# Same operations and fetches in another order on all engines

## The chip, the cores and the metric

One core of a Trainium2 chip runs the kernel. The time is what the device takes for one execution, in microseconds, as the median of several. All five engines work beside each other, each through its own queue in its own order, and wait for each other by semaphores: TensorE (PE in the profile; PEld is its loading of weights), VectorE (DVE), ScalarE (ACT), GpSimd (POOL) and SyncE (SP), which here only issues loads and stores.

## The reference

Two stages, all in float32. First an attention over a sliding window with a bias that falls with distance, for 8 batches, 8 heads, 576 positions and 64 columns a head; then, on its result with the heads side by side (512 columns), a mixture of 4 experts of which each position uses 2. Each expert is itself a causal attention of 64 columns.

```python
scores = scale * np.matmul(q, k.transpose(0, 1, 3, 2))
mask = (rel >= 0) & (rel < 128)
scores = np.where(mask, scores + bias[None], -1000000000.0)
attn = softmax(scores);  x = attn @ v            # then heads side by side: B, 576, 512
logits = x @ w_gate;     topk = the 2 largest of 4;  w = softmax over these 2
for e in range(4):
    q, k, v = x @ wq[e], x @ wk[e], x @ wv[e]
    ye = softmax(causal(scale * q @ k.T)) @ v @ wo[e]
    out += (w of e where e is in topk, else 0) * ye
```

## The kernel before

The attention goes by groups: a group g is a pair of heads of one batch, so there are 32, four to a batch; positions are cut into four tiles of 128 and a tail of 64. For a group PE forms scores (tiles `s`), DVE lays the window together (`copy_predicated`), adds the bias and finds the maximum in one custom operation (`p<-s,tbt`), ACT takes the exponential and its sum, DVE sums and inverts (`tensor_reduce`, `reciprocal` into `r`), POOL or ACT scales `p`, PE transposes it (`t`), DVE or ACT copies it to `pa` (one copy is multiplied by a mask, `pa<-t,tmt`), PE multiplies by the values (`x`), and the result is stored as a rounded part and the rest (`xh`: a copy, then a difference). Groups 0 to 3 at the start are handled in two halves, A (tiles `sA`, `pA`, `tA`, `paA`, `xA`) and B with the tail C (`sB`, `sC`, ...).

The experts' part works on a batch of four groups: projections to q and k (`qk`, stored to `QSm` and `KHm`, again as a part and a rest), to v and the gate (`v`, `lg`), scores (`ms`, tail `msl`), softmax (`mp`), transposes (`mt` to `mpt`), values (`ma` to `AHm` and `ALm`; the tail `mal` to `AHTm` and `ALTm`), and the output projection (`o` to `ot`), which is stored. The weights of all projections are split as well: `WH` is the rounded copy of the staged `wst`, `WL` the difference, by `wprep` (line 1006).

Heads are 64 wide, so many matmuls use only half of the array's columns (the values, `x` and `ma`, two at a time on the two column halves) or half of its rows (scores of the first groups). A change between such a tiling and the full array is a change of array tiling.

The program is first recorded, not issued: `_Rec` (line 188) stands in for the engines, and every call of line 201 on is put into a list. Where two engines could do an operation, `nc.any` (line 195) records both alternatives: copies from PSUM to SBUF (`evac`, line 218: ACT or DVE), rounding and scaling (`rnd`, `scl`, lines 222 and 227: POOL or ACT), differences (`ssub`, line 236: DVE or POOL). `plan` (line 158) then turns the list into the real order. It unpacks the constant `ORDER` (line 39), which holds one entry for every instruction of the whole kernel: twice the number of the operation plus 0 or 1 for the alternative, or a negative number for a fill, a matmul on a zero tile whose result nobody reads (`warm`, line 411). Two matmuls on the two halves of the array make one entry (`_pairs`, line 145). The last lines issue what comes out:

```python
    seq_ = plan(nc.ops, nc.alt) if K["mode"] else nc.ops
    for e, m, a, k in seq_:
        getattr(getattr(tc.nc, e), m)(*a, **k)
```

That is why every row of the profile names line 1276, and why rows are told apart by the tiles they write and read. The order of one engine is the order of its entries; only semaphores tie the engines to each other. Tiles come from pools with a fixed number of buffers, so an entry that writes a buffer waits for the last reader of what was in it.

Loads go mostly through SP: the e tiles (q and k of groups 0 to 7), `vt` (values), `wst` (weights), `mtt` (a mask), from group 8 on `r` and `tl`, and the stores of `ot`. POOL's queue fetches `h` and the copy of `wo`.

Of the kernel before, what the change touches and what calls it, by code (L numbers as in the profile page):

```python
# [19 lines left out]
B, H, S, D = 8, 8, 576, 64  # L20
DM = H * D
E = 4
P = 128
NP_ = H // 2
# [14 lines left out]
    "c-pmjeOzl-m3GcKD<8LTO>Ck`P1>ZAX{bblB^_uJC#gvVZ_<J#l_<Fb78G7V!G@N!V1q&nQ>b7;!9s-!N=BH0npm(w!2yMzprFKp1_gx*dg%)m"  # L39
    "6f8K*-us*cTHAU5dIRJn=j_k5o@cFRZBhYJfxI+%BBLfRU9U{-D9~hgSSoxXLrUQ!Skel0;-o^IxvRChN*ox<mvwDOZM7SD`ibbq%MYuUSF5H!"  # L40
    "{_5h^rRy}sj|<9tryu!~$(FP~`{AF=I_p4}r_$tYRg1sNd$i7CYUp1pfpBT<je^R>hSIM*XmCHoBd>S0zUy&MdO^T&dlK(U@X1e0bk!ZEt5=dd"
    "6(7It_V2X+W#i7~)cnFdcdh38PZrfy7+Q)F!IM|&^M37mIFjvvzu{W7#PPSs(lYDp-PN_m_r9&U>++@D@YEk4aQyDYik-~i&W6U8bTicKxA~M0"
# [1321 lines left out]
```

## Time and profile before

| | us |
|---|---|
| runs | 545.03, 545.17, 545.23 |
| median | 545.17 |
| the profiled execution, its own time | 545.23 |
| its span on the core | 543.5 |
| busy: PE, DVE, ACT, POOL | 532.0, 451.4, 424.7, 348.8 |
| granted clock of PE over the span | 1.00 |

Busy time is a sum over an engine's instructions; that of PE is modelled, as matmuls are pipelined, and bars of DVE overlap the next one by some 0.08 us. A row of the timeline gives the start, the time, the engine, the line, the operation, what it writes and reads with its shapes, how many in succession were put together, and in brackets the idle time of the engine ahead of it with the engine and tile that ended it.

### The profile page before, as it was taken

The page shows a single profiled execution, that of the slowest core. Times are in us where ns is not written, and L with a number is a line of the kernel's source. Part 1 is how long each engine was busy: PE and PEld are TensorE (multiplying, and loading weights), DVE is VectorE, ACT ScalarE, POOL GpSimd, SP SyncE. Part 2 cuts the span into 40 slices and gives each one's busy share as a digit, 9 for nine tenths or more (in the row PEclk, how much of TensorE's full clock was granted, in tenths as well). Part 3 has the DMA queues.
Part 4 walks back from the last instruction along what each step waited for, and adds up shares of the span by engine and source line. Part 5 has one row for each costly group of instructions (what it writes and reads, how often), then busy time and mean ns, then how long its engine had stood idle before and what let it go on. Part 6 is the DMA issues. An engine that isn't in the chain of part 4 may idle for free.

```text
span 543.5 us, 13708 instructions
## 1 busy us (share of the span) xinstructions
PE 532.0 (98%) x4353; PEld 453.9 (84%) x4353; DVE 451.4 (83%) x1945; ACT 424.7 (78%) x1477; POOL 348.8 (64%) x591
## 2 busy tenths in 40 slices
PE   6899999999999999999999999999999999999997
PEld 4688877897898878899788987889789898898875
DVE  4899898989887888898988888878998889866852
ACT  4877888978988888976979769867798977665782
POOL 2644577788766766576596687865669666632640
PEclk9999999999999999999999999999999999999999
DMA  7963424354533547416436354435445240200013
GB/s 201 252 189 109 155 74 145 132 163 160 200 128 98 175 143 239 157 59 199 141 123 201 119 202 149 148 107 175 162 156 169 81 161 24 76 21 2 19 60 98
DMA packets 30376, 72.99 MB, mean 134 GB/s; under 512 B 3168, under 2 KB 11360, under 8 KB 30304
## 3 DMA queue, kind: packets, MB, share of 16 engines
q1 hardware_dynamic: 22752, 42.69, 25.1%
q0 software_dynamic: 6672, 28.84, 16.2%
q8 instruction: 35, 0.57, 0.4%
q10 hardware_dynamic: 880, 0.59, 0.4%
q14 instruction: 37, 0.30, 0.2%
HBM read 62.67 MB, written 9.44 MB: 133 GB/s over the span
## 4 chain that ended last, share of the span: by engine, by line
PE 92%; DVE 3%; DMA 3%; issue 1%; SPq 0%; ACTq 0%; ACT 0%; DVEq 0%
PE qk L1276 19%; PE s L1276 11%; PE v L1276 10%; PE o L1276 9%; PE x L1276 8%; PE ms L1276 7%; PE mt L1276 7%; PE ma L1276 7%; PE t L1276 5%; PE msl L1276 2%; PE mal L1276 2%; PE xt L1276 1%; DMA e<-in_rd 1%; PE mtl L1276 1%; DVE pa L1276 1%; DMA tbt<-in_tb 1%
## 5 line engine op out<-in xcount | busy, mean ns | idle before, releaser
L1276 POOL TENSOR_TENSOR h<-r,h 64x512 fp32r<-64x512 f32 x96 | 122.9, 1282 | 16.7 <-DMA r<-in_rd 9.9
L1276 PE MATMUL qk<-xh,WH 128*128 128x288 f32 (+2 forms) x512 | 123.0, 312 | 0.4 <-DVE ot L1276 0.3
L1276 ACT ACTIVATE p<-p,nm 128x128 f32<-128x128 f32 x252 | 99.3, 396 | 14.4 <-DVE nm L1276 12.8
L1276 PEld LDWEIGHTS qk<-xh,WH 128*128 128x128 f32 x512 | 85.0, 189 | 5.2 <-issue 1.6
L1276 POOL TENSOR_SCALAR mp<-mp,mr,w 128x512 f32<-128x512 f32 (+3 forms) x128 | 76.1, 604 | 16.9 <-DVE mr L1276 9.8
L1276 ACT ACTIVATE mp<-mp,mnm 128x256 f32<-128x256 f32 (+3 forms) x128 | 71.1, 557 | 13.5 <-DVE mnm L1276 12.9
L1276 PE MATMUL qk<-xh,WL 128*128 128x288 f32 (+2 forms) x256 | 76.8, 307 | 0.0
L1276 PE MATMUL s<-h 128*128 128x256 f32 x336 | 72.8, 299 | 0.0
L1276 POOL TENSOR_SCALAR p<-p,r 128x128 f32<-128x128 f32 x131 | 47.4, 368 | 36.6 <-DVE r L1276 13.2
L1276 PE MATMUL ms<-KHm,QSm 128*128 128x256 f32 (+2 forms) x224 | 69.0, 359 | 0.1
L1276 DVE TENSOR_TENSOR pa<-t,tmt 128x512 f32<-128x512 f32 (+2 forms) x84 | 64.3, 773 | 5.6 <-PE t L1276 3.7
L1276 PE MATMUL v<-WH,xh 128*128 128x260 f32 x288 | 65.2, 294 | 0.0
L1276 ACT COPY mpt<-mt 128x384 f32<-128x384 f32 (+1 forms) x84 | 44.1, 534 | 26.6 <-PE mt L1276 25.1
L1276 PE MATMUL mt<-idt,mp 128*128 128x128 f32 x320 | 60.9, 273 | 0.0
L1276 DVE CUSTOM_DVE_ANT_0 mp<-ms,mtt 128x256 f32<-128x256 f32 (+2 forms) x96 | 52.4, 552 | 8.1 <-PE ms L1276 7.5
L1276 PEld LDWEIGHTS s<-h 128*128 128x128 f32 x336 | 53.3, 189 | 3.7 <-PE ma L1276 0.4
L1276 DVE CUSTOM_DVE_ANT_0 p<-s,tbt 128x128 f32<-128x128 f32 x204 | 53.2, 284 | 1.9 <-issue 0.2
L1276 PE MATMUL x<-pa,vt 128*64 128x256 f32 x448 | 51.6, 359 | 0.1
L1276 DVE COPY_PREDICATED s<-mkt,s 128x256 f32<-128x256 int32 (+2 forms) x140 | 45.0, 330 | 6.3 <-PE s L1276 4.4
L1276 PE MATMUL t<-idt,p 128*128 128x128 f32 x252 | 49.7, 273 | 0.1
L1276 PEld LDWEIGHTS v<-WH,xh 128*128 128x128 f32 x288 | 48.2, 189 | 1.9 <-issue 1.3
L1276 ACT ACTIVATE p<-p,r 128x128 f32<-128x128 f32 x121 | 45.4, 396 | 5.0 <-DVE r L1276 3.7
(180 smaller groups left out, 1381.4 us busy)
## 6 DMA issues: line engine op xcount, KB each, us to landing
h<-in_hd POOLq DMA_DIRECT2D x24, 1152.0 KB, 5.8
r<-in_rd SPq DMA_DIRECT2D x24, 576.0 KB, 4.2
vt<-in_vd SPq DMA_DIRECT2D x28, 320.0 KB, 3.8
out<-ot SPq DMA_DIRECT2D x31, 256.0 KB, 3.3
e<-in_hd SPq DMA_DIRECT2D x18, 128.0 KB, 4.4
wst<-in_wall SPq DMA_DIRECT2D x4, 386.0 KB, 5.1
tl<-in_hd SPq DMA_DIRECT2D x24, 64.0 KB, 3.4
out<-ot SPq DMA_DIRECT2D x8, 128.0 KB, 2.4
```

The source lines that it names most:

```text
L1276: getattr(getattr(tc.nc, e), m)(*a, **k)
```

## The change

Only the constant `ORDER` is replaced, a packed text of 99 lines; all code and all operations stay.

```diff
@@ -36,105 +36,105 @@
 ORDER = (
-    "c-pmjeOzl-m3GcKD<8LTO>Ck`P1>ZAX{bblB^_uJC#gvVZ_<J#l_<Fb78G7V!G@N!V1q&nQ>b7;!9s-!N=BH0npm(w!2yMzprFKp1_gx*dg%)m"
...
-    "#iJI*A^6Q46+4lp-s(RMZ*2U({RiTI>2t0n{=dKe2iG*+_5"
+    "c-pmjeOzm2mG1sn`8Z89X-RJwK}k*8#6nG4Vu=lH(uOgdk~V2!3<?!&Q0PE~7TTmG7A#ayuwWAlE%AT@Eli;UmP|oGgMxxWg%K(!+=2rNQ>dVD"
...
+    "b0|A&(9>s+MC;~g!#`^2%hoxo&S?6a<F0O~(*KYDAwivQLA|e6&l7^7|C<i}|EJgg1ypak>H"
 )
```

Unpacked, the list has 6483 entries instead of 6482. The one more is a fill (14 instead of 13; the fills stand among the first 55 matmuls in both). 384 operations take their other alternative: POOL to ACT 123, ACT to POOL 117, ACT to DVE 74, DVE to ACT 62, POOL to DVE 5, DVE to POOL 3. An entry stands at another place of its engine's list for 2877 of 3192 entries of PE, 1470 of DVE, 977 of ACT, 563 of POOL and 94 of SP. On PE the column-tiled runs move as wholes and in parts, mostly by about a microsecond of PE's own work, at most by 18 us later or 8 earlier.

At the start the two lists look like this on DVE (operation, tile written, tiles read; the numbers are places in the engine's list, counted from 0):

```text
place  before                                after
28     minimum pA2 <- sA2                    copy paA <- tA0
29     minimum pA2 <- sA3                    split paA <- tA0,tmt
37     split paA <- tA1,tmt                  copy paA <- tA1
40     tensor_reduce r3 <- sm                tensor_reduce r3 <- sm
41     copy xh1 <- xA1                       reciprocal r3
42     copy WH <- wst0                       difference WL <- wst0,WH
43     difference WL <- wst2,WH              copy WH <- wst3
44     reciprocal r3                         difference WL <- wst1,WH
45     difference xh1 <- xA1,xh1             copy WH <- wst1
50     copy_predicated sB0_1                 difference xh1 <- xA1,xh1
56     difference xh2 <- xA2                 copy_predicated sB0_1
```

ACT gives the copies to paA of tA0, tA1 and tA3 to DVE, and three of its scalings to POOL; three copies to WH come to it from POOL. Its exponentials of one group stand closer together. On PE the transposes of tA3 come ahead of the first sC instead of behind the values xA2. On SP the first 19 loads are the same; then come, before, vt0, vt1, four e2, vt2, vt3, e4, e6, vt4 and so on with mtt at place 43, wst4 at 44 and tl8 at 46; after, tl8, vt0, vt1, e2, mtt, three e2, vt2, wst4 (place 28), vt3, e4, e6, e6, vt4. On POOL's queue the load of h for group 8 comes ahead of that of wo. In the last microseconds the cast of AHTm for the last tail is put on ACT, behind a copy to ot.

## Rows read from the trace of the kernel before

**Rows 1.** The page: busy time of PE with its share of the span and its instructions, and the chain that ended last, by engine.

```profile
PE 532.0 (98%) x4353; PEld 453.9 (84%) x4353; DVE 451.4 (83%) x1945; ACT 424.7 (78%) x1477; POOL 348.8 (64%) x591
PE 92%; DVE 3%; DMA 3%; issue 1%; SPq 0%; ACTq 0%; ACT 0%; DVEq 0%
```

**Rows 2.** Busy time by stretches. Columns: the stretch, its length, busy time and instructions of PE, PEld, DVE, ACT and POOL, the granted clock of PE, the busy share of the DMA engines, and GB/s.

```profile
6.20:20.00 13.80, 11.30 (x65) 8.55 (x66) 10.37 (x62) 10.31 (x44) 7.67 (x18) 1.00 0.95 268
20.00:37.00 17.00, 17.00 (x151) 13.18 (x150) 15.86 (x73) 13.60 (x55) 10.70 (x20) 1.00 0.68 183
37.00:60.00 23.00, 23.00 (x207) 19.12 (x206) 20.92 (x100) 17.86 (x74) 7.13 (x16) 1.00 0.51 153
60.00:84.30 24.30, 23.85 (x194) 18.98 (x193) 22.79 (x104) 19.66 (x75) 18.62 (x37) 1.00 0.33 107
...
100.00:540.00 440.00, 439.28 (x3627) 379.88 (x3623) 367.31 (x1551) 348.30 (x1181) 290.79 (x476) 1.00 0.39 127
```

**Rows 3.** The chain of waits, 83 to 86 us: start, us, what.

```profile
84.08 0.09 DVE ws L1276
...
84.23 0.70 PE ms L1276 x2
```

**Rows 4.** Timeline of PE, 74.4 to 78 us.

```profile
74.97 1.77 PE L1276 MATMUL x<-pa,vt 128*64 128x256 f32 x16
76.67 0.38 PE L1276 MATMUL ms<-KHm,QSm 128*128 128x256 f32 x1
76.98 0.45 PE L1276 MATMUL xt<-pa,vt 128*64 128x64 f32 x8
```

**Rows 5.** Groups of instructions of DVE with shapes kept apart: busy time, mean ns of one, idle time before them.

```profile
L1276 DVE COPY pa<-t 128x256 f32<-128x256 f32 x9 | 3.7, 414 | 0.0
...
L1276 DVE TENSOR_TENSOR WL<-wst,WH 128x256 fp32r<-128x256 f32 x2 | 0.8, 414 | 0.0
```

**Rows 6.** Timeline of DVE, 8 to 20 us: the reductions that wait.

```profile
10.79 0.16 DVE L1276 TENSOR_REDUCE r<-sm 128x4 f32<-128x8 f32 x1 [0.91 <-ACT pA L1276]
...
16.09 0.16 DVE L1276 TENSOR_REDUCE r<-sm 128x4 f32<-128x8 f32 x1 [0.68 <-ACT pA L1276]
...
18.79 0.16 DVE L1276 TENSOR_REDUCE r<-sm 128x4 f32<-128x8 f32 x1 [1.08 <-ACT pA L1276]
```

**Rows 7.** Timeline of ACT, 8.5 to 21 us: two exponentials.

```profile
10.28 0.38 ACT L1276 ACTIVATE pA<-pA,nmA 128x128 f32<-128x128 f32 x1
...
18.25 0.41 ACT L1276 ACTIVATE pA<-pA,nmA 128x128 f32<-128x128 f32 x1
```

**Rows 8.** The chain of waits from 0 to 40 us (first row) and the timeline from 19.6 to 23.5 us (the others).

```profile
12.35 7.33 DMA e<-in_rd
...
19.82 0.56 PE L1276 MATMUL sC<-e 128*128 128x192 f32 x2 [0.69 <-DMA e<-in_rd]
...
21.96 0.76 DVE L1276 COPY_PREDICATED sB<-mkt,sB 128x256 f32<-128x256 int32 x2 [0.50 <-PE sB L1276]
...
22.62 0.66 PE L1276 MATMUL tA<-idt,pA 128*128 128x128 f32 x4
```

**Rows 9.** Timeline of DVE, 49 to 67 us: waits for PE, and one for ACT.

```profile
49.13 0.43 DVE L1276 COPY_PREDICATED s<-mkt,s 128x256 f32<-128x256 int32 x1 [0.21 <-PE s L1276]
...
56.90 0.49 DVE L1276 COPY_PREDICATED s<-mkt,s 128x128 f32<-128x128 int32 x2 [0.22 <-PE s L1276]
...
59.90 0.76 DVE L1276 COPY_PREDICATED s<-mkt,s 128x256 f32<-128x256 int32 x2 [0.41 <-PE s L1276]
...
62.97 0.16 DVE L1276 COPY lg<-v 128x4 f32<-128x4 f32 x1 [0.78 <-ACT v L1276]
...
65.69 0.29 DVE L1276 COPY_PREDICATED s<-mkt,s 128x128 f32<-128x128 int32 x1 [0.29 <-PE s L1276]
...
66.70 0.29 DVE L1276 CUSTOM_DVE_ANT_0 p<-s,tbt 128x128 f32<-128x128 f32 x1 [0.25 <-PE t L1276]
```

**Rows 10.** Issues on SP's queue, 18 to 32 us, the sB matmuls of group 2 on PE, and from the page the median time from issue to landing of such a load (last column).

```profile
18.03 0.60 SPq L1276 DMA_DIRECT2D e<-in_rd  x1
19.70 0.60 SPq L1276 DMA_DIRECT2D e<-in_hd  x1
...
31.28 0.33 SPq L1276 DMA_DIRECT2D vt<-in_vd  x1
...
27.14 1.13 PE L1276 MATMUL sB<-e 64*128 64x256 f32 x8
...
e<-in_hd SPq DMA_DIRECT2D x18, 128.0 KB, 4.4
```

**Rows 11.** Timeline of all engines, 536.5 to 543.6 us.

```profile
536.99 0.22 DVE L1276 CAST AHTm<-mal 128x64 fp32r<-128x64 f32 x1 [2.61 <-PE mal L1276]
...
537.54 0.37 ACT L1276 COPY ot<-o 128x256 f32<-128x256 f32 x1 [0.59 <-PE o L1276]
...
538.06 0.29 PE L1276 MATMUL o<-WOH,AHTm 128*128 128x256 f32 x1
```

**Rows 12.** Timelines of POOL, 15 to 18.5 us (first two rows), and of DVE (the last).

```profile
15.49 0.77 POOL L1276 TENSOR_SCALAR WH<-wst 128x256 fp32r<-128x256 f32 x2 [0.56 <-DMA wst<-in_wall]
...
16.97 1.00 POOL L1276 TENSOR_SCALAR WH<-wst 128x260 fp32r<-128x260 f32 x2
...
17.29 0.41 DVE L1276 TENSOR_TENSOR WL<-wst,WH 128x256 fp32r<-128x256 f32 x1
```

More of the change, by code (lines that the diff above doesn't have):

```diff
@@ new lines @@
+    "1qJ24@4I(6oYVPZ?jJY5kmT(B?)PJ@=UMAn>lgqGKwc`h*r;-+Bq@S<sv47RL0?tY9!^eWWvO|ptdKpVO{oZV+lJ)cBK`DSRzvQ<^jdf9dg0n&"
+    "$7GTJy-(N1R>qy&`fx#w20kV*rWJqu$v}Y-D)j>{*(a!{vwbp;KkH`?=X~hF!omq#o31xUntZaWdXA!Ac;e{>*IU1Qi2Bg+rv!4r#rv(F%#PGb"
+    "uX)@KpSWYt|5zf0Ua#s6-dpaS&1@`cPQ2~!O$N}n78&P%`{J$NFG^B+gYD{2V^grQ8cu(3dn5eupAGlDnU$VkcT{9v|6H?5@~)sJWQeO-Gqi-v"
+    ")`sQ}KQrSIl>w}JmP|go^=mK2l<4<9@J5p%$v@xxz$de{`Op+hZ7;G`Wj=6QUGtA_2%5G2m_Xk_0~E^q<5MZ?YjxEFH6hJZ&00$8dORymNd?f3"
+    "?Euszy3z{);+5!1PFeAQ<&o@*^s8-q6;FIxp^4Gxt8=b>xr(h9N&Agebs9rr&q!Kof4HGquRmxC0+baS68&Dt&IDEJWK+Jm?6G^r*~x(pxbV*G"
@@ new lines @@
+    "a6;#r`qr1r)4%XhNYdVN8z^L|I8eo%9BLA*k`oE6&rI%Yss@Lr5;{SfG&TZ|Y}(0inKw=0*rC0Dd}S%&`a2d!4Y$6&wLWm|Z4PsbqY)s+)LQD>"
+    "eDPw(@m^E)64WG*LQSH<mJX2NLhnqe1HSXBGb=Dt6Yo%Fo2~BnSRI;ua>i4nH#)@$b*cqt_5Rc;0?-pruWsZOz~V}RX8#Dx@yf)Kj|r8o%G>X-"
+    "DW*%S*W$MOQZL*H;cwoOyPTjAS-oj7D*&>zIhZcB!nC5a8a&eJjS=W-hu7bLPzz*c2U|inzF?C=Ot>&PsiHsp?VrN_ku1<7Q?yJhLH|HoQbPb-"
+    "r_j)7U4>U)Z0g?GoO|pyp<`-$Z})(O;m)3+(Y6qbXdMZ^__X)BdqmpIdb2&Rpi40*Z4F3zx(_UJkjP<LGpE+|TH@<+x8s)^lk0P`q1-pKo7SF>"
+    "Z5(mcsZGA}&7H2iaJjGCa&qT~`viB}gHQh8jk~6mJNva;dgErLuVH^;Xeax^%@M8Dd?fRX&K9Tktr|}DYZqOR9PDb>)MREuXJ=3WDb3!UWU+py"
@@ new lines @@
+    "VXhBudj#x;TBYpzkEO*m8~l5ou5g2|f85hkYfAM@heuM55|^cs33skUerTFN{xqy1|93CgOM}qcB@Kj^*JcM4^4TKj?kkur>r<P>^1--{8*etq"
+    "a<x!Vd}7;KU0L5+&aQ`J>b>9lo6&g#tq`+*GC7kFkFK3&C1^5DD)`Lj)H(zRb*jYr-8TzMY%Oa&F|pl!`#0RA*2xsCxXqGQEN&@07%?VVWo?EA"
+    "Q{<_;Hih>dYz<B+cjZl*gbY_nVIxdin@x)=@Vj>b%186#lG?>d`4;KVzgvFN7F&P#EF*3@)Fn3Ol!?F<nc6a2or>gX>$c}KtK65l0=BiD={Z}4"
+    "@IHxL0Y-b+Gi40)fAM+{4HP#IA@kY$MsnTbePUbp9{le=NGz4QRyZC`hhs-L<HO%C^7Oc4(@(nljw#5v^;r<vT$$M-DXWZ!Q>(eXWLmb?q$z{s"
+    "{A`5Ryn>vW<ucDV|Ef27jH+@UNIkh)Yu5NwAnPf?L{so*pY|bS{Op~kYOl20mkw&5b78lOE!ZnN4VJ;~!Q_nghhG9X1+TxXT)YbQTK{6HF%Uvi"
@@ new lines @@
+    "w>K*gBia)tAfjABbWz4n4l9<EO<>Ogun&b{aA#p8tkg(Mb3<Y2{N~=&>0mHk+7D|}Z2%LI)<9{!uTres%G)Z|R8GBj;bgGLl2+GPToz|9%24Y("
+    "pSnB#XKzG`9{tbeVsm`+$c3MmRul#|+d2R`d&B*%jQWm|vC4nFIoVtNm9M7T-u{ho$g{nNtU&b+By5TyPIVZNj3u0`9wwGFEsA5}5hi2`mw(bS"
+    "yE0c=QCcytNO|Nx=ONeK+~7=?2G^mnZm=;U>qn1|&c~1T4~LWqYIi|S?r&-Jn7s@If`kf~KKj<n%CM!h!WyHs23jp?W;U&N1DW+3cV$^*MwQd("
+    "4t9L%zKNgwGgKO-sVQD5BKq`4?oX-KXH;+6?I<`ydHvqD)D)WSf$cr;u4yNVZuwgCL>A1Oon>*>wL;<dOk2yZerKhj$1ILlrVW4elW1J==n;xn"
+    "$5dUTO#`dUr#0R&=i~pDQc+p4djens!?wlZZC$p=4q!b#dB!MO-s&CLjEz}7ST6gIUj?pxC-bAX&r%DA)~$7m2H-@z9WymPH5+d~JQ>;h@Vn`@"
@@ new lines @@
+    "4o}ZVo^>khF3HIet$ndQ^|;{Doqhf8)<F9YE|g^b?O972o8<0Wjx}31=V5f{B(b6{9eJxMXcs$!?Iqx}F7EVB#Ku%nl?sUQD>qCCBXKH#bekb@"
+    "+hPEnyAd{@f9j^UJoR3Qh$^n!DX!crMd7v~@9SR#3!A={paE9Ai84&GLz`ekkv%6rx#$=7)xzA-?i{G5lIJz`f=lKhfN)LdcdKu-0JwA2Q_$H1"
+    "@U`bpI|{z@s;9`Ei@3msPH${|G--S)(eT)-;3*nXnUW1jCRRKJiH3SavCJ&UF@y@cl9HOrHCfH>B+&TEQD|V*{(;`X?hXIo@av!LhVMQg?vj-S"
+    "T62nL%6*l=xX@t=n0z~4zeilw;IHvHMXk;W*QDPxyPz1KiHUWmfn@gpAPsEt?!IXh_2(cNZ4>tTc3=6S8Z-%T+~AjkOrcQ1sc{Ziom`SAUQ9HU"
+    "JN|OV)Z|$A()>W@BhM#5u&FsRY!GkX_j?yBotqxF!{$!TGe4^_7Ua3E|I(17%q@4=+gWjB!lmr%+;%Fna<xgBJ@<SGoG9;0`k=k5XV78pbd=VG"
@@ new lines @@
+    "J9-WqC6&6x6)ja&3%A_Xn-+>w#UZ8`r@EU}Co!>bDn3!`jth#1?T(Bbk@O&<2Wk2*sxMZQHrDiISZCr-w|@DAPODr)%(Y8`(xLUBC1^jCDLX95"
+    "4aT7_JRdYBw&cQde+8T0?(tcuWM_7xZE&Ty%r@R!B8fk}`?E2+CHv$|=XdUPX4!xLy0x#{a^3IJi**G}!Gw@)=GWgZF3^jUitDqL4b7G`eOK9b"
+    "tv9r~Av-d`u-6Z%`_DXe(BPWL?wr~`8uz)jCsu9ZLDPh-$Xx|XO=VgB28&8rK3v<Y)NJm^5$+C8?te)~nTJO6SN_irM{KEw@qx61WTQ^O&Mcza"
+    "p0&^3E|NA$(%`dqD#5Y>{o8x`HJwr+)+SBQN#v1<*#((m(iuO$6q$%SumU@wqvl1Tt)v)GCXVds)BIk46;yi*OMH;!oX$13nR8Dvm$df^w%n1R"
+    "?K6LddSvXP-dF^UmHYnWSu3A$=H!c{Gn*<fCn-SPJv?ZySgNm?g#*yGA`t-QreMsamnK2puvd^ONz1ONvO54_rlNc{Js~q&3nxj7^);<0lA0a1"
@@ new lines @@
+    "CHzmH44Zoj2MzThc<LP#6!mF)01eFueupP^S7CvD*r2u!H(S_Vqdq?grXRZ}v4EYs_YZpG`j%vIi|FCQB@N8O4X=SRFi<I*v%u*@BsHb35d~Sb"
+    "E&z%l)2=u>b88)3a*^~ee??iKZncCJcaN6^bjR$(zg_Hr@!3|GZOA|MHO?;Nm73POBqay&dFdDLkJT!wG;>|;<zAl;pi)tS>{Ta?i7oei;0qZ$"
+    "OXa?8#mayEAx=F}-4YM2NK_??M@A~t;Z}Ek4vJ8=^kWL0<=5}P@*2uB(}(+sTOy<VrrVBKyTUZbMzS*}D7L+49Cq}E%^j!eZ!baX$mnSxrY}(B"
+    "sh^yijufYEX%^+*x~|(Q%PjI}YQOz2?%Z+z=dZCtWFp&Bv|%3avj2_23D+@_e^dm{R-{jxN+GpjXw;Q4G*C)a91aaT>@ffL-x%AfV`7bZ({`Us"
+    "AyJrCWJi&eE$AJ9<@att@yAt{x)Bh!b+~gu7MbYK&e<AcO6x~VKGBR*otin(I$Ni;R=B?RgK*u1^%M?4l0FWh?Sm6}IR)m$ShKTv`pfrQeDJrg"
@@ new lines @@
+    "($8$}RLb&q65~y>`d*jl$M?o1H?K9^{G6v}T;=GrrN@*=tw#;bt7-BQW&R47t)2cPz3dZDn=AS|yS!tFExGRe2i{K7PUPmL2bw1e<}+9^Ol5!d"
+    "y{gXUWssQvaC<`5TwHmdOe94a@dMY{9qLuf29ki11KX1iOM=d!z9q0qVl5`iAo7c6E!EMdUyg-8|FP!~>5h@H{n1O;+77zQhDJ@@eYxrxu%zuC"
+    "%rC9V6l=?RV}{DWipw7P6557$!Ch55Xk3~Hzc-_``)Hloa%Q*=Cp;sXIF(u#bL9N@mtp<iFXe>?^1}Vlgrc{n@nr4ByGvm8;-6sqzPq}56`?>A"
+    "G&el_kaH?#7$8A2c$x*;(%44m7uCY9ZEVD7$Q-bmpL}w&W5n+bHZ;38vYnIG%6A^3_Qe_m<o2%RH6+=O6HLxv6N06I<fWO#MDhO7GD=hBsZK+#"
+    "TeYCp+4_$F#l?)Gtw5`2IBO`;0L!U$joQkuJh?MI)!qe<J=vnusjK!*TU-t#bllo9@qU`+`VUzLU^j29XnwG9@?fxWd}?}bIiVy7vsq|1INq>X"
@@ new lines @@
+    "#op<+E+L^XFZ^Y(?8Z0ObN^}XQ8b^j8PP0bt!dbq1+xWZdaa%sEXgh%9d7Fw+8>Zrt3wf~Z%C5}N!fLWrLWz3A_ccY4oI0nXK{=Jl$z0@srKXy"
+    "mk}wN5qEB@ExmU;gkag(6It3B8kJ-Z?;fmg!Q@;yl*~W%^it;`l%dLIFcxK)OTYX1!yo-Idze~LAR7=54ul%kHaje7Ucaqy4+a%7Iem1ezid-8"
+    "9}c-Y)4M0O4h!IhH@maJ7J~k8dsm0q+CE-%h$5FO!)gJT+?)OF^OKbI!fTrgu~64I3v;Ki+vCtC4V5f9)($`X(@HI(jH5|jnGsqJI-G#AG3a#}"
+    ";#P0#h(SA36I6eMy)`rYK<3d^rqwyDrpQ!n)uc{Ss3?WdaY0C)p-(g>8tQgBY(?@%?s)5x#0uu3BYWL~dLE9tD=BTa1XWbifdad4HIeoB^a(nP"
+    "F)?3nl;}1<9g$yp$+PB#8MexiIz33=R5ZU-STer^?H)1xb|M-gksq{&S#hx~yblMv%__Y!>&wqNa<aD8CpA5=tFt(cp88{1O?^|a&T5t&2epN<"
@@ new lines @@
+    "2ld*n^|U2dXZGUSJV;{U!UwCZBMF+*3gh8eWUOXtcHz5kT8@glQUY_k!$YGGXr0|fqFKCg91l6xx#@Vd)*+clC^@ws!J_SRcRC=W<FSh+gJ1l7"
+    "Tij^4a_Y;^PR?W>YA58=KYC#>2Qmxu?VX7AuD1RnZ3Be6`-*3}P%&SgF@At9gC|>_<wU7#a$z|%IXUC=jW12K90tdC)KCP41EWZMWM(JiWmeB+"
+    "7(V{x`kMNhtu_e1d!P8;hjvp^HLI1Wrz*n&QZ6DXN+&=0IXwF8UhjZyX0igxZPEycQYVL8thglyJTWTh9=7;UAyQclw)9i!2T?)f%ojyQorN%5"
+    "sI~sX4aI3m#XbGoUG1SxbZB_vm81DRxc=7%Ald+P{u&^dAjP+tq#r{^h-AI^%@Xeh=(AC_YerET)o=m*)b2rLbz4difKo3Wu50(@wNXy5asxTK"
+    "xZa24EmTKZRsx4ocf~^gL}m5YpPNj#rMHbwMT}kJQ~O#mt84Qe*e4=cPT$V>03c$c)Hed76by|nf*HwGS?=B`oMtH4!GkFn30rr6{KVJpxp<dN"
@@ new lines @@
+    "J~9xeIq4theC-t}s?~$+c#dv<AppV3x`y(`m<_8WYjwj8?Z%XR_eQ_o`p0XJZh0_XsV;Em<`py~4D_PP8oJ{;0<Ftyb?J}XT$|F|0Im&4rYgI2"
+    "Fe$3YcdhKN^_q)nQJmO3QXM;0a;>AbGg34z54iUN7UiC^4a`e+XBMjP!D<dX@M1g+H~C7f)2h?IKaia;9{a}|8lQfz;uzIvkra@G%~Hr|z4IQ3"
+    "Q92UkG5Yk`g~@O}geQ+?d#k<ayE&~Xg<<ISEw7DqJ5s7EUCQ+BLUlkcyZe^U-Sng9?IqowqH({>qW#oYYU5%fX&aTXRAu!{(^On~|Asonzwx(w"
+    "hYL$KTWUA`Wyqn3`}UKP<e58YV}eP#mRD&r$Wtm?|N8a`3e=~N0HXZ@Pmx4E2)m9QoAkj4+fH2m#Yku$)JPa5yR+BhXHF}cCr=_()-($>QV(^b"
+    "r(gjws@pY^f&85Qur~z;%6<LE0}uYkH8-wI#Gueqr<ik>gRLM@u7Z?(L$S2r(Z?YrHB)6Ot*}T<civOizYxx-)2tqJz+%0#3zq#~d9kA(U@A@2"
@@ L138 @@
+    "77^M+-wR2Rh{F&|Y=`W`oNEHpd}xk#ISC_Jf*yv;ywS>)3xHHqp-^PTGX)jR0(=3@D@sm7k*a|xE;d@P(pMGFG<DX3;=5wJ!i&}dELV<m5uCZQ"
+    "8GEjyz-yoXrnyaD)d7!gl8W{_qgSGW>wIVLtaVDA`(XICH+5#4vv%G2>ABL2lxQ?fN5$Y(&29FwPdKh!Im2bLl12w}c2vF}7cHEw5WT!&zpDLB"
+    "b0|A&(9>s+MC;~g!#`^2%hoxo&S?6a<F0O~(*KYDAwivQLA|e6&l7^7|C<i}|EJgg1ypak>H"
 )
```

137 lines of the change are left out of this document (40 added, 97 removed).

## The prediction

> **What bounds the kernel now.** I read the page first. PE is busy for 98% of the span, and of the chain that ended last 92% is PE and 3% is DVE [rows 1]. So time can only be won where PE stands idle. The windows say where that is [rows 2]: from 100 to 540 us PE lacks 440.00 - 439.28 = 0.72 us, from 37 to 60 us nothing that this view shows, from 6.2 to 20 us it lacks 2.50 us. Busy time hides something here, because a PE that restarts between two short stalls is still counted as busy. Therefore I laid PE's matmuls end to end, each with the time it takes undisturbed (the distance of starts within an unbroken run), and compared that count with the real starts. PE is behind its count by 14.1 us at 20 us, by 24.9 us at 89 us, and by 37.7 us at the end; the last 12.8 us are spread over 450 us in pieces of about 0.1 us, the 10.8 us in the middle over only 69. The chain of waits agrees: it runs through DVE up to 84.17 us and through PE from 84.23 us on [rows 3]. So the kernel has three stretches. Up to about 20 us the head waits for loads and for the first softmaxes; from 20 to 84 us DVE is the engine whose work sets the end (busy 15.86 of 17.00, 20.92 of 23.00 and 22.79 of 24.30 us); behind it PE alone does.
>
> **What is in the change.** Only the packed order differs, so I unpacked both and set them side by side on every engine. The set of computations is the same but for one more fill matmul (14 for 13). 384 operations that may run on either of two engines go to the other one; DVE gets 1511 instructions instead of 1497, ACT 1029 for 1035, POOL 579 for 587. PE's order moves nearly everywhere, though mostly by one microsecond of its own work; changes of its array tiling go from 149 to 148. At 76.67 us a full-array matmul of 256 columns stands between two column-tiled runs: 0.31 us to the next start, where a 256-column matmul of the run before takes 1.77 / 16 = 0.11 [rows 4], so a pair of changes costs 0.20 us, one costs 0.10. One change fewer is -0.1 us, which I leave inside the error. PE's total, counted as above, is otherwise equal to 0.03 us.
>
> *Part 1, DVE before the gate.* Queued on DVE before the copy on sB at 21.96 us stand 12.01 us of work before and 13.70 us after, so +1.69 us. It is made of ten operations more and five fewer: three WL differences more and two fewer, three copies of transposed probabilities to paA (formerly ACT's), two WH copies more and one fewer, a v copy, an xh copy more and two fewer. By the rows the WL differences and the copies to paA take 0.41 us each [rows 5], of which some 0.08 lie over the next instruction. Fully on the path this would be +1.69 us. What hides it: DVE is idle for 13.80 - 10.37 = 3.43 us between 6.2 and 20 us [rows 2], of which 0.91, 0.68 and 1.08 us are reductions of the row sums that wait for ACT's exponentials [rows 6]. In the new order these exponentials stand earlier on ACT. The one at 10.28 us moves from the eleventh to the seventh place; the last of its group has 1.24 us of ACT work ahead of it instead of 2.13 (-0.88). For the reduction at 18.79 us the last exponential is the one at 18.25 us with 8.85 us ahead [rows 7]; afterwards it is another with 7.35 (-1.50), while DVE's own work ahead of the reduction falls by 0.39. So the first wait goes (0.91 - 0.88), the last goes (1.08 - 1.50 + 0.39), and the middle one stays (ACT -1.02, DVE -0.94). That gives back 0.88 + 1.08 = 1.96 us against +1.69. DVE now reaches the copy at 21.96 us with 0.50 us to spare, since it waits for PE's sB [rows 8]. In the new order it would be there 0.27 us earlier, and still waits. And PE's sB cannot come sooner: the sC before it waits for the load that is issued at 12.35 us and takes 7.33 us, to 19.68 [rows 8], and the first 19 loads on SP stand in the same order. I take 0. The bounds are +1.19 (no wait shortens: 1.69 less the spare 0.50) and -0.44, by moving the four transposes of tA at 22.62 us, 4 x 0.11 us, ahead of that sC into time in which PE waits for the load.
>
> *Part 2, DVE from the gate to 84 us.* The work queued there grows by only 0.07 us. What can go is waiting: DVE is idle for 1.14, 2.08 and 1.51 us in the three windows, 4.73 us in all [rows 2]. For each matmul that DVE waited for I counted how much PE work and how much DVE work lies between the gate and it in either order; DVE work more, or PE work less, gives the matmul a longer lead. Five waits lose all by this count: at 49.13 us (0.21, lead +1.36), 56.90 (0.22, +1.63), 59.90 (0.41, +1.29), 65.69 (0.29, +0.85), 66.70 (0.25, +0.62) [rows 9]. Together 1.38 us. The wait of 0.78 us at 62.97 us is for an ACT copy and is not judged. Looking for the opposite, of the 177 DVE operations that follow a matmul between 22 and 100 us only one (at 99.9 us, where PE leads) gets a lead shorter than the spare it has now. Ends: -4.73 if every wait closes, and 0 if the lead is eaten elsewhere. I take -1.38 + 0.07 = -1.3 us. Ahead of the matmul that last waits for DVE PE has 62.8 us of work instead of 62.6, so 0.2 us less is left behind it: -0.2.
>
> *Part 3, the fetches.* 94 of 158 loads and stores on SP change place. Two loads (64 and 205 KB) go ahead of the e loads that are issued at 18.03 and 19.70 us and serve the sB at 27.14 us [rows 10]. At the 268 GB/s of that window [rows 2] 269 KB are 1.0 us; with two more issues of some 0.4 us each about 1.8 us. The second of them would land at 19.70 + 1.8 + 4.4 (the median for its kind, [rows 10]) = 25.9 us, so 1.2 us of cover is left; if it lands as late as the load at 12.35 us did, PE waits 1.7 us there. The load into wst4 goes from place 44 to 28 on SP and blocks the queue until a buffer is free, but the load at 31.28 us [rows 10] waits for its own buffer in both orders, and nothing that is held between them is used before 37 us. I take 0.
>
> *Part 4, the tail.* One cast of AHTm moves from DVE, where it starts at 536.99 us, to ACT, behind the copy to ot at 537.54 us that takes 0.37 us; the matmul that needs it starts at 538.06 [rows 11]. So it would start at about 537.85 and take 0.2, and the difference ALTm comes after it: between +0.1 and +0.3 us, I take +0.2.
>
> **Sum.** 0 - 1.3 - 0.2 + 0 + 0.2 = -1.3 us against the profiled execution, whose time was 545.23 us (543.5 span and 1.73 around it); the median of the runs shown is 0.06 lower. Forecast: 543.9 us.
>
> *A rule weighed against a row.* Two POOL copies to WH took 0.77 us at 15.49 us and two took 1.00 us at 16.97 us, while DVE formed a WL difference from 17.29 us on [rows 12]. The Trainium skill (SBUF — State Buffer, section on the two separate sides, "Reading the diagram") says that DVE and GpSimd share a port pair as an exclusive lock, and that a DVE operation with two SBUF inputs keeps a GpSimd operation that reads SBUF out for its whole length, or the reverse. The row agrees for POOL (+0.23 us); by the rule the one WL difference more on DVE would cost POOL another 0.23, or DVE up to the 0.4 us of the POOL copy that got there first, and the sum would then be -0.9 instead of -1.3 us.
>
> **The rivals.** *A, the waits move.* DVE and PE wait for each other from 20 to 84 us; a wait that closes at 49 us may open as one of the next, since PE comes no sooner than DVE's results let it. For it: the idle time of DVE there is in short waits all over, 4.73 us of which I can trace 1.38. Against it: the leads are longer than the waits by 0.4 to 1.4 us each. Then 0 + 0.07 - 0.2 + 0.2 + 0 gives 545.3 us, and 545.2 is about the median. *B, the extra copies are not absorbed.* Place: DVE between 8 and 22 us. If the reductions still wait for ACT, which also takes over three WH copies from POOL, DVE starts the copy on sB late by 1.19 us (at 23.15 instead of 21.96; from 22.2 us on it counts), PE's next matmuls wait for it and so the loop keeps its waits: 545.23 + 1.19 + 0.07 - 0.2 + 0.2 = 546.5 us, and 547.0 if the spare 0.50 us goes too. For it: ACT's exponentials depend on PE's sA and DVE's minima as well, not on their place alone. Against it: two thirds of DVE's work added there comes off ACT. *C, the e loads* land last at 27.14 us: +1.7 on the forecast, 545.6 us.
>
> **How the numbers follow.** Changes within 0.2% (1.09 us) can't be told from none. Forecast 0.53, with its own range 542.4 to 545.0 (0.41 below 544.08, 0.12 within). A 0.23 (0.03 faster, 0.20 same), C 0.06 (same), B 0.18 (slower). Faster 0.44, same 0.38, slower 0.18. The range is 542.0 (-1.4 -0.44 and some of the untraced 3.35 us) to 546.6.
>
> **What would show it.** Right: in the profile after, the copy on sB starts within 0.3 us of 21.96 us; the reductions' first and last waits are gone; the five waits are gone; the chain goes over from DVE to PE some 1.3 us earlier than 84.2. Wrong: that copy later than 22.5 us, PE waiting for an e load before the sB of group 2, or DVE idle for over 4 us again between 20 and 84 us with the crossing at the same time.

## The result, and the profile after

The changed order takes 548.27 us (median of 6, 547.11 to 549.51) against 545.1 us for the kernel before (6 runs, 544.88 to 545.53): a ratio of 1.0057, 95% interval 1.004 to 1.0074. That is 3.2 us slower, outside the stated range and on the side to which 0.18 had been given. The six times fall apart into 547.1 to 547.7 and 548.8 to 549.5; the profiled execution is of the first kind, 547.11 us with a span of 545.3 us.

The page of the changed kernel, the rows that answer to [rows 1]:

```profile
PE 532.3 (98%) x4354; PEld 452.8 (83%) x4354; DVE 461.9 (85%) x1959; ACT 422.1 (77%) x1471; POOL 347.4 (64%) x583
...
PE 89%; DVE 5%; DMA 3%; ACT 1%; POOL 1%; issue 0%; SPq 0%; ACTq 0%; DVEq 0%; POOLq 0%
```

DVE has 14 instructions more, yet is busy 10.5 us longer. The stretches (columns as there), as in [rows 2]:

```profile
6.20:20.00 13.80, 11.14 (x70) 7.52 (x69) 11.60 (x64) 10.47 (x45) 10.20 (x22) 1.00 0.94 259
20.00:37.00 17.00, 16.61 (x138) 12.81 (x140) 16.42 (x69) 10.54 (x45) 8.94 (x18) 1.00 0.82 243
37.00:60.00 23.00, 22.92 (x212) 19.14 (x210) 21.72 (x106) 19.47 (x80) 7.76 (x16) 1.00 0.46 149
60.00:84.30 24.30, 24.15 (x195) 19.10 (x193) 22.30 (x97) 19.82 (x74) 15.83 (x33) 1.00 0.23 70
...
100.00:540.00 440.00, 438.80 (x3622) 378.92 (x3622) 375.45 (x1565) 344.42 (x1174) 291.16 (x473) 1.00 0.40 128
```

These windows do not say where 1.9 us went. The count of the prediction does: how far PE is behind its own matmuls laid end to end, at four points of that work (about 29, 56, 89 and 538 us of the execution), an estimate worked out from the traces, good to some tenths of a microsecond, since it rests on what is taken as a matmul's undisturbed time:

```text
                       13 us   36 us   64 us  500 us  of PE's work
before                 16.12   19.70   24.86   37.85
changed                16.69   20.92   25.44   39.51
difference             +0.57   +1.22   +0.58   +1.66
```

So 0.6 us is lost in the head, the stretch bound by DVE gives nothing (8.74 us between the first and the third point before, 8.75 after), and another 1.1 us goes where PE alone was thought to set the pace. The rest to 1.9 is the tail and the time around the span.

**The head.** The timelines of DVE and of POOL in the changed kernel:

```profile
17.74 1.00 DVE L1276 CAST WH<-wst 128x260 fp32r<-128x260 f32 x1 [0.51 <-DMA wst<-in_wall]
18.66 0.41 DVE L1276 TENSOR_TENSOR WL<-wst,WH 128x256 fp32r<-128x256 f32 x1
18.99 0.49 DVE L1276 CAST WH<-wst 128x256 fp32r<-128x256 f32 x1
...
20.19 1.48 DVE L1276 TENSOR_TENSOR WL<-wst,WH 128x256 fp32r<-128x256 f32 x2
...
23.09 0.76 DVE L1276 COPY_PREDICATED sB<-mkt,sB 128x256 f32<-128x256 int32 x2
```

```profile
17.53 1.05 POOL L1276 MEMSET KHm<- 64x1152 f32 x1
18.67 0.66 POOL L1276 TENSOR_SCALAR WH<-wst 128x256 fp32r<-128x256 f32 x1
19.30 0.77 POOL L1276 TENSOR_TENSOR WL<-wst,WH 128x260 fp32r<-128x260 f32 x1
...
20.51 0.89 POOL L1276 TENSOR_TENSOR WL<-wst,WH 128x256 fp32r<-128x256 f32 x1
```

The DVE copy to WH at 17.74 us takes 1.00 us, where the same form took 0.29 before, and ends 0.16 us after POOL's memset (17.53 + 1.05 = 18.58). The two WL differences at 20.19 us take 1.48 us together instead of 0.8 and end 0.27 us after POOL's WL (20.51 + 0.89 = 21.40). The time lost is not shown as a wait in brackets; it lies inside the row, in its length, here called the bar. Summed over the head's WH and WL operations on DVE, the bars are 1.65 us longer than undisturbed (0.29 for a copy, 0.41 for a difference), in the trace of before 0.08 us. The copy on sB starts at 23.09 instead of 21.96 us [rows 8], and it no longer waits for PE.

**Behind 100 us.** The gate of each batch ends in small DVE operations. One of them adds 1e-9 to a sum of 128x5. The timeline of the changed kernel at 143 and at 404 us:

```profile
143.69 1.29 POOL L1276 TENSOR_TENSOR h<-r,h 64x512 fp32r<-64x512 f32 x1
...
143.88 1.12 DVE L1276 TENSOR_SCALAR ws<-ws 128x5 f32<-128x5 f32 x1
...
145.65 0.33 PE L1276 MATMUL t<-idt,p 128*128 128x128 f32 x1 [0.30 <-DVE pa L1276]
...
404.10 1.30 POOL L1276 TENSOR_TENSOR h<-r,h 64x512 fp32r<-64x512 f32 x1
...
404.32 1.11 DVE L1276 TENSOR_SCALAR ws<-ws 128x5 f32<-128x5 f32 x1
...
406.43 0.72 PE L1276 MATMUL s<-h 128*128 128x256 f32 x4 [0.73 <-DVE mr L1276]
```

An addition that takes 0.17 us when it is alone lasts until POOL's operation on h is over (143.69 + 1.29 = 144.98; 143.88 + 1.12 = 145.00), and PE falls back by 0.46 and 0.90 us behind the two. The groups of instructions say it in one number, before and after:

```profile
L1276 DVE TENSOR_SCALAR ws<-ws 128x5 f32<-128x5 f32 x8 | 2.6, 325 | 0.1
L1276 DVE TENSOR_SCALAR ws<-ws 128x5 f32<-128x5 f32 x8 | 4.6, 573 | 0.1
```

Five of the eight are long in the changed kernel (1.12, 1.00, 0.43, 1.11 and 0.46 us). The kernel before has two (1.02 and 0.55 us), and three more held operations of its gates, 0.28 to 0.73 us long. Its longest, from its timelines of POOL and DVE:

```profile
206.36 1.28 POOL L1276 TENSOR_TENSOR h<-r,h 64x512 fp32r<-64x512 f32 x1
...
206.65 1.02 DVE L1276 TENSOR_SCALAR ws<-ws 128x5 f32<-128x5 f32 x1
```

PE falls back by 0.54 us behind it.

### The profile page after: what moved, and what is told of

Its sections match the earlier page's. It is cut to its first block, busy times and chain, and to the rows that moved or that the text cites. A ratio compares the mean times of both kernels' runs of the same rounds, so it can differ in the third digit from the quotient of the medians.

```text
span 545.3 us, 13684 instructions
## 1 busy us (share of the span) xinstructions
PE 532.3 (98%) x4354; PEld 452.8 (83%) x4354; DVE 461.9 (85%) x1959; ACT 422.1 (77%) x1471; POOL 347.4 (64%) x583
## 4 chain that ended last, share of the span: by engine, by line
PE 89%; DVE 5%; DMA 3%; ACT 1%; POOL 1%; issue 0%; SPq 0%; ACTq 0%; DVEq 0%; POOLq 0%
PE qk L1276 18%; PE s L1276 10%; PE v L1276 10%; PE o L1276 9%; PE x L1276 7%; PE mt L1276 7%; PE ms L1276 7%; PE ma L1276 7%; PE t L1276 4%; PE msl L1276 2%; PE mal L1276 2%; PE mtl L1276 1%; DMA e<-in_rd 1%; DVE pa L1276 1%; PE xt L1276 1%; DMA tbt<-in_tb 1%
## 5 line engine op out<-in xcount | busy, mean ns | idle before, releaser
L1276 POOL TENSOR_SCALAR mp<-mp,mr,w 128x128 f32<-128x128 f32 (+3 forms) x128 | 76.6, 610 | 21.5 <-DVE mr L1276 12.5
L1276 PE MATMUL qk<-xh,WL 128*128 128x288 f32 (+2 forms) x256 | 77.9, 309 | 0.0
L1276 ACT ACTIVATE mp<-mp,mnm 128x384 f32<-128x384 f32 (+3 forms) x128 | 71.0, 557 | 6.5 <-DVE mnm L1276 4.8
L1276 PE MATMUL s<-h 128*128 128x256 f32 x336 | 71.4, 299 | 0.9 <-DVE mr L1276 0.7
L1276 PE MATMUL ms<-KHm,QSm 128*128 128x256 f32 (+2 forms) x224 | 66.6, 356 | 0.0
L1276 ACT COPY mpt<-mt 128x512 f32<-128x512 f32 (+1 forms) x78 | 41.4, 536 | 24.4 <-PE mt L1276 24.0
```

## The experiments

Theory L: a DVE operation that works from SBUF to SBUF (copies, two-input differences, small additions and comparisons) stands still as long as POOL has an operation running there, and the new order puts more of these side by side, at places where PE waits behind them. The rivals: S, all of the loss is made in the first 89 us; W, it is the mere number of DVE's added operations; and that the places of PE's matmuls make it. In the rows of edited kernels the line is not 1276, as the edit moves it. The first four ran on one chip, beside 29 runs of the kernel before (median 545.7 us).

**The change once more.** No edit.

> The changed order as it is, once more, so that the other three can be held against it on the same chip. In its first profile two additions of a constant on DVE to ws (128x5, usually 0.17 us) took 1.12 us at 143.88 and 1.11 us at 404.32 us, each until the POOL operation on h that ran then (1.29 us) had ended, and PE stood 0.30 and 0.73 us behind them. Theory L (these and similar small DVE operations are held up by POOL, at places that the new order makes worse): 547 to 549.5 us, with one to five such long rows in the profile, at the same places or others. Theory S (the loss is made in the first 89 us, by DVE's added copies): the same time, but with PE 1 us or more behind the kernel before at 89 us and no further loss after it.

547.63 us (8 runs, 547.01 to 548.84), ratio 1.0038 [1.0026, 1.005]. In its profile the same additions take 1.12 us at 145.6 and 1.09 us at 405.7 us, so they are no accident of one execution; in the head the bars are 2.0 us too long. This profiled execution was of the upper kind, 548.48 us, for a reason of its own: PE waited 0.66 us at 39.99 us for an e load, the only profile of a changed order in which that happened.

**Head alone, rest alone.** The 959 operations with which the kernel before starts (up to 88 us) in one order, the others in the other.

```diff
-order = after
+order = [x for x in after if x in first_959] + [x for x in before if x not in first_959]    # head
+order = [x for x in before if x in first_959] + [x for x in after if x not in first_959]    # rest
```

> The order of the change for the 959 operations that the kernel before starts with (up to 88 us), the order and engines of before for all others. Theory S: as slow as the change, 547 us or more. Theory L: only what the first stretch costs, +0.5 us by the first profile of the change (PE at its offset of 88 us was 0.5 us later), so 545.6 us, and none of the long additions of the change at 144 and 404 us.

> The reverse: the first 959 operations (up to 88 us) in the order of before, all others in the order and on the engines of the change. Theory S: 545.1 us, as before. Theory L: the change's loss less the half microsecond of its start, 546.5 to 549 us, and long additions to ws or comparisons to cnt in the profile.

547.24 us for the head alone (ratio 1.0026 [1.0013, 1.004]), 546.95 us for the rest alone (1.0022 [1.0011, 1.0034]). Both are slow, 1.5 and 1.25 us above before, and together about the change's own 1.9 us on that chip and the cost of the seam (in the head's profile PE loses some 0.5 us in the 5 us behind the cut). The head alone came out where theory S had it; theory L was 1.6 us too low there, since it had taken the 0.5 us of one profile. But S had 545.1 us for the rest alone, which is slow as well and has the long additions at 147 and 407 us, so S falls.

**Without the additions.** The eight additions of 1e-9 are left out.

```diff
+        if m == "tensor_scalar" and len(a) > 2 and a[2] == EPS:
+            continue
         getattr(getattr(tc.nc, e), m)(*a, **k)
```

> The changed order without the eight additions of 1e-9 to the sum of the gate's exponentials (ws, a sum of at least 1); nothing else is left out. Theory L: 0.7 to 1.5 us faster than the change on the same chip (two waits of PE, 0.46 and 0.90 us, go). Theory S: the same time within 0.3 us, since eight times 0.17 us on an engine that is not the bound are worth nothing.

546.86 us (12 runs), 0.8 us under the change, with times from 545.0 to 547.4 us. The two waits of PE are gone. But the profile (547.12 us) has a new one, larger than either:

```profile
313.70 0.78 POOL L1278 DMA_DIRECT2D h<-in_hd  x1 [1.27 <-DMA r<-in_rd]
313.86 2.05 DVE L1278 TENSOR_TENSOR G<-lg 128x80 f32<-128x80 f32 x1
...
314.51 1.28 POOL L1278 TENSOR_TENSOR h<-r,h 64x512 fp32r<-64x512 f32 x1
...
316.47 0.47 PE L1278 MATMUL ms<-KHm,QSm 128*128 128x512 f32 x1 [1.52 <-DVE nm L1278]
```

The gate's comparison G, 0.23 us when alone, stands for 2.05 us: through the 0.78 us in which POOL issues the load of h, and through the h operation behind it. PE waits 1.52 us. Here, I thought, are the two groups of times. In the first profile of the change G was not held up, though it met the issue there too, at about the same distance of 0.15 us:

```profile
314.29 0.78 POOL L1276 DMA_DIRECT2D h<-in_hd  x1 [1.24 <-PE mt L1276]
...
314.44 0.23 DVE L1276 TENSOR_TENSOR G<-lg 128x80 f32<-128x80 f32 x1
```

So whether G is held differs from one execution to the next; what decides it no trace shows.

**The memset back, the engines of WH and WL back.** Both are edits to the changed order; these two, and further down the gates' edit of the order of before, ran on another chip (before: 12 runs, median 545.3 us), on which the change itself was not run.

```diff
-POOL: ..., pA, memset KHm, WH, WL, ..., pB, ...
+POOL: ..., pA, WH, WL, ..., pB, pB, memset KHm, ...
```

> The changed order with one entry moved: POOL's memset of half of KHm (64x1152, 1.05 us) goes from ahead of the WH copies at about 18 us back to where the kernel before has it, behind the first scalings of pB. DVE's list is untouched. Theory L (a DVE operation from SBUF to SBUF stands still as long as POOL has a store or load running there): the DVE copy to WH that ran beside this memset and took 1.00 to 1.07 us takes 0.3 to 0.4 us, the copy on sB starts 0.4 to 0.8 us earlier, and the time falls by 0.3 to 0.8 us to about 547.3 us. Theory W (it is the number of DVE's added copies that made the head late): that copy keeps its length and the time stays within 0.2 us of the change.

```diff
-engine of the 24 operations on WH and WL as in after
+engine of the 24 operations on WH and WL as in before      # 11 change
```

> The changed order in which the operations that form WH and WL run on the engines that the kernel before uses; 11 of 24 go back (five from DVE to POOL, three from POOL to DVE, three from ACT to POOL), their places in the order stay. Theory L and theory W both give back most of the head's loss, 0.8 to 1.5 us, as DVE has two such operations less; they differ in the bars: by L what is lost in DVE bars of over twice the usual length goes from 1.7 to 2.0 us to under 0.8 us, by W the bars were not the point and the gain is 0.7 us, the time of the two. If POOL's longer list makes the matmuls wait for WL instead, the time stays.

Neither is faster than the change (ratios of 1.0057 and 1.0038 in its two sets of runs): 548.33 us (1.0049 [1.0035, 1.0064]) and 548.85 us (1.0058 [1.0045, 1.0071]). The gains expected, 0.3 to 0.8 and 0.8 to 1.5 us, did not come; what the second run had named as a way to none, that PE waits for POOL's longer list, did. The bars do what L says. With the memset gone, the copy that had taken 1.07 us takes 0.49; the lost time of the bars falls from 2.0 to 1.24 us, and to 0.76 us with the engines back, where the copy on sB starts at 21.87 us, on time. But each edit puts a wait in the place of the one it takes away. In the first the memset now stands ahead of a scaling for which PE waits, in the second POOL's longer list makes PE wait for a WH copy:

```profile
31.19 1.06 POOL L1268 MEMSET KHm<- 64x1152 f32 x1
...
33.47 0.33 PE L1268 MATMUL tB<-idt,pB 128*128 128x128 f32 x1 [0.67 <-POOL pB L1268]
```

```profile
24.15 0.78 POOL L1268 TENSOR_SCALAR WH<-wst 128x256 fp32r<-128x256 f32 x2
...
24.61 0.38 PE L1268 MATMUL qk<-xh,WH 128*128 128x256 f32 x1 [0.83 <-POOL WH L1268]
```

In both profiles G was held for 2.05 us at 315 us, too. These two runs settle how the bars come about; what the bars cost they leave open.

**The gates' small operations off DVE.** The additions left out, the comparisons for cnt on POOL; once in the order of before, once in the changed one (the latter on a third chip, 23 runs of before with a median of 545.73 us).

```diff
-        nc.vector.tensor_scalar(cnt, cnt, 2.0, None, op0=ALU.is_lt)
+        nc.gpsimd.tensor_scalar(cnt, cnt, 2.0, None, op0=ALU.is_lt)
...
+        if m == "tensor_scalar" and len(a) > 2 and a[2] == EPS:
+            continue
```

> The same edit to the order of the kernel before, where a ws addition took 1.02 us at 206.65 us and PE stood 0.54 us behind it. Theory L: 0.4 to 0.6 us faster than before, about 544.9 us. Theory W: the same as before within 0.2 us.

> The changed order without the eight additions of 1e-9 to ws, and with the eight comparisons that give cnt moved from DVE to POOL at their places; nothing else is left out. The same edit gave the order of before 1.44 us. Theory L: PE's waits at 144 to 147 us (0.46) and 404 to 407 us (0.9) go, 1.3 us less than the change where the difference G at 314 us is not held up, so about 546.5 us, and up to 1.6 us more in executions in which it is; what is left against the edited order of before is the head's 1 us. If the loss behind 100 us came from the places of PE's matmuls, the time stays within 0.3 us of the change, 548 us.

The order of before gets 1.44 us faster: 543.86 us, ratio 0.9971 [0.996, 0.9982], more than the one wait of 0.54 us had promised, and below both kernels. The changed order comes down to 545.64 us, 2.0 us less than the change on the first chip (the medians of before on the two chips agree: 545.7 and 545.73), ratio 1.0004 [0.9993, 1.0015]. Between 64 and 500 us of PE's work the profile now loses 12.14 us, the edited order of before 11.95, before 12.99 and the change 14.07. So behind 89 us the places of PE's matmuls make no difference worth the name; the held operations of the gates do.

An edited kernel has the same list of matmuls as its original, so the starts can be set against each other one by one, and then the gain comes in steps. In the changed order PE gains 0.57 us at the addition of 143.88, 0.25 at that of 208.79, 0.9 at that of 404.32 and 0.2 us at that of 509.19 us, all four of them long; the fifth long one (275.14 us) and the three gates with short ones give 0.13 us at most. In the order of before it gains 0.56 us at 206.65 us and 0.5 us at 263.38 us, where a comparison for cnt stood for 0.51 us, and 0.17 us at most at any other gate. By theory W, the mere number of operations taken off DVE, all gates would have given about the same; W falls for the gates.

The times of the changed order still stand in two groups, eight at 545.25 to 545.73 us and four at 546.4 to 547.3.

**POOL kept quiet while G is formed.** On top of the gates' edit, two entries of POOL go behind the first G addition of batch 4. This run and the last one shared a fourth chip.

```diff
-POOL: ..., dma h, h<-r,h, G<-G, ...
+POOL: ..., G<-G, dma h, h<-r,h, ...
```

> As the run on the gates alone (whose times fell into 545.2 to 545.7 us in most executions and 546.4 to 547.3 in four of twelve), with two entries of POOL moved: the load of h and the first h operation that stand ahead of the gate's first G addition of batch 4 go behind it, so that POOL has nothing running from SBUF while DVE forms G and Q there (314 us). Theory L: the upper group of times goes, a median of about 545.5 us with hardly any over 546. If the two groups come from elsewhere, from the loads at the start for one, both stay, in about the same shares.

545.38 us, and all eleven times lie between 545.20 and 545.74: no upper group. That the move did it is likely, not shown: the run without it was on another chip, and the kernel before, too, was over 546.2 us in 6 of 23 runs there and in none of 21 here. The profile shows POOL waiting and G unhindered:

```profile
313.79 0.23 DVE L1270 TENSOR_TENSOR G<-lg 128x80 f32<-128x80 f32 x1
314.11 0.20 POOL L1270 TENSOR_TENSOR G<-G 128x5 f32<-128x5 f32 x1 [1.75 <-DVE G L1270]
314.59 0.77 POOL L1270 DMA_DIRECT2D h<-in_hd  x1 [0.27 <-POOL G L1270]
```

**The head's copies on ACT.** On top of the gates' edit, DVE's three WH copies of the head go to ACT, without and with the move of the two POOL entries.

```diff
-                ("vector", "tensor_copy", (o, q), None) if x else ("scalar", "copy", (o, q), None),
+                ("scalar", "copy", (o, q), None),
```

> As the run on the gates alone, and the three DVE copies to WH of the head (two added by the change) go to ACT at their places in the order, where ACT was idle for over 4 us at 19.4 to 23.6 us. Theory L: DVE loses 0.9 us of work and up to 1.4 us of standing still beside POOL there, the copy on sB starts at 21.8 to 22.2 us (as early as the load lets it), and 0.6 to 1.0 us go on top: 545.7 us. If the head is late for another reason (ACT's xh copy behind its own WH copy, or POOL's WL), the copy on sB comes earlier and the time stays that of the gates alone.

> The same move of two entries, with the three DVE copies to WH on ACT as well (that run had times from 544.6 to 547.6 us, half of them above 546). Theory L, and the head late by DVE's bars: about 544.8 us, 0.7 us under the run without the copies on ACT, and hardly any over 545.8 us. If the copies on ACT gained nothing, 545.5 us as the other.

Without the move 546.11 us (12 runs, 544.59 to 547.64), so nothing by the median; with it 544.56 us (544.09 to 545.22), 0.82 us under the run with the copies on DVE (545.20 to 545.74 on the same chip), ratio 0.9984 [0.9976, 0.9993]. Without the move the spread of 3 us had hidden such a gain. DVE's WL differences in the last kernel:

```profile
17.34 0.75 DVE L1270 TENSOR_TENSOR WL<-wst,WH 128x256 fp32r<-128x256 f32 x2
...
19.71 0.41 DVE L1270 TENSOR_TENSOR WL<-wst,WH 128x256 fp32r<-128x256 f32 x1
...
22.42 0.76 DVE L1270 COPY_PREDICATED sB<-mkt,sB 128x256 f32<-128x256 int32 x2
```

The copy on sB starts at 22.42 us instead of 23.65 in its neighbour without this edit; the lost time of the bars is 0.30 instead of 2.02 us, and PE is 0.86 us less behind at 13 us of its work (16.37 against 17.23), 0.84 at 64. How much of this the bars cost by themselves is open, as the copies took their own work of some 0.9 us off DVE too.

## Why the prediction was wrong

**What bounds the kernel.** The three stretches were read rightly, but one conclusion was not: that behind 84 us PE alone decides and nothing on another engine matters. PE lacked only 0.72 us there [rows 2], which tells what before lost, not how near the next loss stood. Two additions held for 0.95 us more were enough for 1.36 us of PE. The group of these additions in the trace of before (eight in 2.6 us, a mean of 325 ns with one row of 1.02 us) was there to be read.

**Part 1, the head: the step that failed.** "I take 0" rested on DVE reaching the copy on sB 0.27 us earlier. The waits did shrink, if by less than worked out: the reduction at 16.53 us waits 0.46 where three had waited 2.67, but three new waits of 0.24 to 0.61 us came, and DVE's idle time from 6.2 to 20 us fell from 3.43 to 2.20 us, by 1.23 and not 1.96. The number of operations was right as well. Mis-sized was the time of one: a WH copy or WL difference on DVE, taken at its undisturbed 0.29 to 0.41 us, took up to 1.00 us beside POOL. The bars that change length cost 1.65 us more in the profiled execution and 2.0 us in four others of this head. The copy started at 23.09 to 23.7 us; rival B had named 23.15 us, the place and nearly the price (1.19 us; measured 1.13 here), though by the reductions, which was not how. Moving the copies, with their bars and their own work, gave back 0.82 us in whole runs; the head alone cost 1.5 us with the seam, so about 1.0 without it.

The rule weighed there (the Trainium skill, SBUF — State Buffer, "Reading the diagram") was the right one, applied to the wrong list. It was priced for one WL difference more, 0.4 us at most, from a row in which POOL was the loser. The traces agree with it in what loses, the one that starts second: in the thirteen profiles 50 of the gates' additions and comparisons (cnt, G) and the head's WH copies and WL differences began on DVE while POOL had 0.15 us or more left of an operation on h or WL, and all 50 stood, to end 0.03 to 0.29 us after it. The prediction had taken it for operations with two SBUF inputs alone; copies and additions with one were held here as well (1.00 and 1.12 us). Not every meeting costs: beside POOL's operations with one input, shorter ones, 33 of 48 stood, and of some 1,190 reductions and reciprocals on DVE that began beside POOL, SBUF to SBUF too, none. The list to go through would have been every other DVE operation from SBUF to SBUF in the whole kernel, with what POOL runs at that time in either order.

**Part 2, -1.3 us: failed, measured 0.** The five waits for PE are gone (the operation of the last now waits 0.17 us, for POOL), but not, it seems, because PE's results came earlier: DVE comes 1.1 us late from the head and can find them ready. A wait that goes since the waiter is late gives nothing back. And two other waits for PE have come, in DVE's timeline of the changed kernel:

```profile
43.64 0.76 DVE L1276 COPY_PREDICATED s<-mkt,s 128x256 f32<-128x256 int32 x2 [0.44 <-PE s L1276]
...
60.86 0.43 DVE L1276 COPY_PREDICATED s<-mkt,s 128x256 f32<-128x256 int32 x1 [0.76 <-PE s L1276]
```

With the head mended (the last run) the same stretch takes 8.57 us of lag instead of 8.74, so the reordered waits were worth 0.2 us at most, which is within the error of the count. Rival A, the waits move, was right here. The chain goes over from DVE to PE at 82.36 us, 1.9 us earlier, which I had put down as a sign of the gain; it was none, since a wait for POOL at 86.25 us follows.

**Behind 89 us, counted as -0.2: failed.** Measured +1.08 in the profiled execution, and some 1.5 us more where G is held (PE waits 1.52 us there). No step of the prediction looked there.

**The fetches and the tail held, nearly.** No profile shows PE waiting for the e loads of sB of group 2; one in ten shows 0.66 us for those of s4, which SP issues after wst4. In the tail, AHTm's cast sits on ACT behind the copy to ot as foreseen (539.21 and 0.37 us, then 539.48); the span grew by 1.8 us where PE was 1.66 us late at 500 us of its work, so the tail cost 0.14 us; predicted +0.2.

**How the sum really reads.** Head +0.8 to 1.0, DVE's stretch 0, behind it +1.1 or, with G held, +2.6, tail +0.2: 2.1 to 3.8 us, and the runs gave 2.0 to 4.4 (547.11 and 549.51 against 545.1). That G is what lifts the upper group of the change itself is not shown: three profiles of edited kernels had it held (547.12, 549.43 and 548.76 us), but the one profile of the change from its upper group (548.48 us) had the e load instead.

## What to carry to other kernels

When work moves between DVE and POOL, or past each other on them, don't price an operation by its undisturbed row: list what both engines run from SBUF to SBUF at that time, reductions and reciprocals aside, and let the one that starts second wait for the other to end. A tiny operation on an engine that is not the bound can hold the one that is, if a long one on POOL is in its way; leaving out or moving sixteen such (543.86 us) was worth more than either order. And a wait that has vanished from the trace is a gain only if the waiter was not late.

## What was not expected of the hardware

POOL's mere issue of a DMA can hold a DVE operation with two SBUF inputs: G stood from 313.86 us through an issue that ended at 314.48 and the h operation that ended at 315.79. It did so in three of the eight profiles in which G began 0.11 to 0.16 us after that issue; in the other five it took 0.23 us. A POOL memset, which reads nothing, held a DVE copy until it ended (at 18.58 us, the copy from 17.74 to 18.74).

One such meeting can go either way from one execution of a program to the next: with the gates' edit the times stand in two groups some 1.6 us apart; after the move of two entries, on another chip, they differ by 0.54 us, and by 1.13 us with the copies on ACT.

The run with the rest alone was profiled in an execution of 549.6 us in which PE waited 1.46 us for a load at 20.9 us and the granted clock then fell to half (1.2 of 2.4 GHz) for some 3 us; its median is not touched by that. By stretches, with the granted clock third from the end:

```profile
20.00:22.00 2.00, 1.07 (x7) 0.87 (x7) 1.52 (x6) 0.98 (x3) 1.46 (x4) 0.96 1.12 228
22.00:24.00 2.00, 2.00 (x10) 1.17 (x12) 0.51 (x3) 0.49 (x2) 1.69 (x3) 0.50 1.08 227
```
